# Local attention and a channel mix on one core: scores at the front of a slot, attention products behind the second key block, and TensorE's order as written

## The chip, the core and the metric

The kernel runs on one core of a Trainium2 chip. A core has a matrix engine (TensorE, PE in the rows), engines for elementwise work (VectorE, DVE; ScalarE, ACT; GpSimd, POOL) and SyncE (SP), whose queue issues the DMA transfers here. Each runs its own instructions in order and waits on semaphores for the others. The metric is the time of one execution in microseconds; lower is better.

## What is computed

Chunked local attention with a few memory keys, whose output goes through a token-shifting channel mix. Everything is float32, for 4 sequences of 768 tokens, 8 heads of 64 (512 channels) and a hidden width of 1024.

```
for each chunk of 32 queries:            # keys: 16 left, 32 own, 8 right, 8 memory = 64
    a = softmax(0.125 * q_c @ k_full.T)
    out_c = a @ v_full
x  = out, heads side by side             # (4, 768, 512)
xk = mu_k * x + (1 - mu_k) * x_prev      # x_prev: the token before
xr = mu_r * x + (1 - mu_r) * x_prev
k  = max(xk @ w_k, 0)
y  = sigmoid(xr @ w_r) * (k * k @ w_v)
```

## The kernel before

The work is cut into 12 units u of 256 tokens, each of two tiles of 128 tokens (tiles 2u and 2u+1). Each unit passes these blocks on TensorE, named here as in the code's tables:

- **s**: the scores of both tiles, 128 small products (line 465). VectorE takes the maximum and subtracts it, ScalarE takes the exponential, VectorE sums and normalizes.
- **a**: weights times values, one block for a tile (line 642), 64 products for the two. From unit 3 on (MOVED) the weights come to it by way of DRAM: VectorE transposes them in 32x32 squares (eT, line 708), SyncE stores them (eD, line 715), and four transfers load them into aTz (line 719). This is in `move`. ScalarE then copies the result into xT.
- **g0, g1**: the sigmoid's products (line 1141), and **h0 to h3**: the key products xk @ w_k (line 1252), 24 products each. Each operand is split into a high and a low part in a shorter float type, so each product is three: high by high, low by high, high by low. VectorE makes the mixes from the difference df of neighbouring tokens (lines 773 and 784); a cast gives the high part xh, a subtraction the low part xl (line 805). The mix for g is made first, the mix for h second.
- **p1 to p7**: the products with w_v (from unit 2 on), by a scheme of seven products instead of eight. Their operands (high parts ah, low parts al) are made of sums and differences of squared ReLUs. They gather in three banks: x (p1, then p2), z (p7, then p4) and y (p6, then p5, then p3). Between two products of a bank VectorE reads it. Three of these reads matter here: **u2** reads y after p6, and p5 waits for it; **c21** reads z after p4; **c22** reads y after p5, and p3 waits for it.

A **slot** u, as the word is used below, is the stretch of TensorE's work that holds h and p of unit u. It also holds g and a of unit u+1 and s of unit u+2.

What sets the order: the program doesn't write it out. Each operation goes into a `Plan` with its engine or alternatives, a cost and what it depends on. `te_order` gives each block of TensorE a due time by a written sequence. Then `Plan.turn` places the operations one by one on a modelled clock. For TensorE it takes only the first in the written sequence until STRICT (420) operations are placed. From then on it chooses among the next LOOK (400), so later blocks of TensorE can pass each other. The other engines' operations are placed among these, wherever the modelled clock has them first. A transfer's result counts as there DLAT (2.0 us) after its cost. The planner has no part in the run: it only fixes each engine's order. From about unit 3 on the order of TensorE that results is not the written one: h0 of the next unit stands ahead of p3, and p2 ahead of p5 or of h0.

Of the kernel before, what the change touches and what calls it, by code (L numbers as in the profile page):

```python
# [24 lines left out]
KT = DM // P  # L25
FT = DFF // P
# [1 line left out]
NEG = -3.0e38  # L28
TINY = 2.0**-112
LOOK = 400  # L30
STRICT = 420
EASE = 0.1
TURNS = 3
WHOLE = ("g0", "g1", "v0")
OWN = (1,)
PARTED = (1,)
LEAD = "s0.0.0 s0.0.1 s0.1 t0 t1 a0 s1.0 a1 h0.0.0 h0.0.1 h0.1.0 h0.2.0 h0.3.0 s1.1 h0.3.1 g0.0.0 g0.1.0 g0.0.1 h0.3.2 h0.3.3 g0.1.1 t2 t3 v0.0.0 a2 a3 v0.1.0 s2.0 v0.1.1 v0.0.1 h1.0.0 h1.0.1 h1.0.2 h1.0.3 h1.1.0 h1.1.1 t4 t5 h1.1.2 h1.1.3 a4 a5 v1.0.0 g1.0 g1.1 v1.0.1 g2.0 s3.0 g2.1 v1.1.0 v1.1.1"
UTOK = 256
FAST = 2
MOVED = 3  # L40
ROWS = [(0, 0, 1), (0, 1, 1), (1, 0, 2), (2, 0, 2), (3, 0, 2)]
QPU = UTOK // P
QKW = NPAIR * NJ * (CHUNK + NK)
VWW = NPAIR * NJ * D
HOP = {"pe": 0.22, "dve": 0.16, "act": 0.16, "pool": 0.16, "dma": 0.1}
SELF = {"pe": 0.0, "dve": 0.1, "act": 0.0, "pool": 0.1, "dma": 0.0}
DLAT = 2.0
# [25 lines left out]
class Slot:  # L73
    def __init__(self, tag):
        self.tag = tag
        self.users = []


class Op:

    def __init__(self, alts, fn, deps, new, use, due):
        self.alts = alts
        self.fn, self.new, self.due = fn, new, due
        self.deps = [d for d in deps if d is not None]
        self.eng = self.end = None
        self.rank = due if alts[0][0] == "pe" else None
        for s in list(new) + list(use):
            s.users.append(self)  # L90


class Plan:
# [4 lines left out]
        self.ops = []  # L98
        self.bufs = bufs

    def op(self, alts, fn, deps=(), new=(), use=(), due=1e9):
        fixed = isinstance(alts, tuple)
        if fixed:
            alts = [alts]
        o = Op([(a + (False,))[:3] for a in alts], fn, deps, new, use, due)
        o.seq, o.fixed = len(self.ops), fixed
        self.ops.append(o)
        return o

    def dues(self):  # L110
        for o in reversed(self.ops):
            for d in o.deps:
                e, c, _ = min(d.alts, key=lambda a: a[1])
                d.due = min(d.due, o.due - c - HOP[e] - (DLAT if e == "dma" else 0.0))

    def place(self, o, free, held):
        ready = [(d.end, d.eng) for d in o.deps]
# [44 lines left out]
    def turn(self, goal, ease):  # L162
        for o in self.ops:
            o.due = goal[o]
        self.dues()
        free, held, todo = {}, {}, {}
        for o in self.ops:
            todo.setdefault(o.alts[0][0], []).append(o)
        for q in todo.values():
            q.sort(key=lambda o: (o.rank if o.rank is not None else o.due, o.seq))  # L170
        done = []
        while len(done) < len(self.ops):
            best = None
            for e, q in todo.items():
                for o in q[: 1 if e == "pe" and len(done) < STRICT else LOOK]:
                    p = self.place(o, free, held)
                    if p is not None:
                        key = (p[1] + max(0.0, o.due - p[1]) * ease, o.due, o.seq)
                        if best is None or key < best[0]:
                            best = (key, o, p)  # L180
            _, o, p = best
            if o.rank is None and ease:
                o, p = self.filler(o, p, todo[o.alts[0][0]], free, held)
            _, t, eng, cost, port = p
            o.eng, o.start = eng, t
            free[eng] = t + cost
            if port:
                free["port"] = t + cost
            o.end = t + cost + (DLAT if eng == "dma" else 0.0)
            for s in o.new:  # L190
                held.setdefault(s.tag, []).append(s)
            todo[o.alts[0][0]].remove(o)
            done.append(o)
        done.sort(key=lambda o: (o.start, o.seq))
        return done


def te_order():

    nu = B * S // UTOK  # L200
    seq = [tuple([x[0]] + [int(n) for n in x[1:].split(".")]) for x in LEAD.split()]
    for u in range(1, nu):
        a, b = 2 * u + 2, 2 * u + 3
        g = [("g", u + 1, c) for c in range(QPU)]
        h = [("h", u, f) for f in range(FT // 2)]
        if u == 1:
            h = [("h", u, z, k) for z in range(2) for k in range(KT)]
        v = [("v", u, c, n) for c in range(QPU) for n in range(2)]
        n = 1 if u == nu - 2 else 2
        t = [("t", a), ("t", b)] * (u + 1 < MOVED)  # L210
        early = [("s", u + 2, 0)] * (u >= FAST)
        if u + 1 <= MOVED:
            seq += h[:n] + t + early + h[n : n + 1] + [("a", a), ("a", b)] + h[n + 1 :]
        else:
            seq += h[:1] + [("a", a), ("a", b)] + h[1:2] + early + h[2:]
        if u >= FAST:
            v = [("p", u, n) for n in (1, 7, 6, 4, 5, 2, 3)]
            if u >= nu - 2:
                g = [("g", nu - 1, u - (nu - 2))]
            if u == nu - 1:  # L220
                v = v[:3] + [("p", u, 4, 0), ("p", u, 5), ("p", u, 4, 1), ("p", u, 3), ("p", u, 2)]
            seq += v[:2] + g + v[2:]
            continue
        seq += v[:1] + [("s", u + 2, 0)] + g + v[1:]
    seq = list(dict.fromkeys(seq))
    last = {"t": B * NQT, "a": B * NQT}
    seq = [x for x in seq if x[1] < last.get(x[0], nu)]
    due, t = {}, 6.0
    for x in seq:
        assert x not in due  # L230
        due[x] = t
        t += PE_COST[x[0]] * (0.66 if x[:3] == ("h", 0, 0) else 0.33 if x[:3] == ("h", 0, KT - 1) else 1.32 if x[:2] == ("h", 0) else 0.5 if x[:2] == ("h", 1) else 1.32 if x[1] == 0 and f"{x[0]}{x[-1]}" in WHOLE else 1)
    return due
# [3 lines left out]
def local_attention__then__channel_mix(  # L237
# [24 lines left out]
    def sb(tag, shape, name, dt=F32):  # L262
        return work.tile(shape, dt, tag=tag, name=name, bufs=bufs.get(tag, 1))
# [19 lines left out]
    op = plan.op  # L283
    T = {}

    def copy(e, dst, src):
        if e is nc.scalar:
            e.copy(dst, src)  # L288
        else:
            e.tensor_copy(dst, src)  # L290
# [4 lines left out]
    qts = [(b, i) for b in range(B) for i in range(NQT)]  # L295
    units = [(b, u * UTOK) for b in range(B) for u in range(S // UTOK)]
    NU = len(units)
    due = te_order()
    chunks = [(w_k, wk_hl, k) for k in range(KT)]
    chunks += [(w_r, wr_hl, k) for k in range(KT // 2)]  # L300
# [309 lines left out]
    def attention(t, o_n, e):  # L610
# [39 lines left out]
        def f_x(e):  # L650
            if c == 0:
                x = T["xT", u] = sb("xT", [P, KT, 1 + UTOK], f"xT{u}")
                if units[u][1] == 0:
                    nc.gpsimd.memset(x[:, :, 0:1], 0.0)
                else:
                    nc.scalar.copy(x[:, :, 0:1], T["xT", u - 1][:, :, UTOK : UTOK + 1])
            copy(
# [42 lines left out]
    def move(u, o_n, e):  # L700

        X, M = NK // CHUNK * 2, NG // 2

        def f_turn():
            T["eT", u] = sb("eT", [P, NG * NK], f"eT{u}")
            nc.vector.transpose(
                T["eT", u].rearrange("p (x m q) -> p x m q", x=X, m=M),
                T["e", u].rearrange("p g k -> p (g k)").rearrange("p (m x k) -> p x m k", m=M, x=X),  # L710
            )

        def f_out():
            T["eD", u] = dram.tile([P, NG * NK], F32, tag="eD", name=f"eD{u}")
            nc.sync.dma_start(T["eD", u], T["eT", u])

        def f_in(x):
            s, z = x // 2, slice(CHUNK * x, CHUNK * (x + 1))
            nc.sync.dma_start(
                aTz[z, s].rearrange("p i n -> p (i n)").rearrange("p (j n) -> p j n", j=NJ),  # L720
                T["eD", u].rearrange("(j p) (x n) -> x p j n", j=NJ, x=X)[x],
            )

        ts, az, ds = Slot("eT"), [Slot("aT"), Slot("aT")], Slot("eD")
        o_t = op(("dve", 1.2), f_turn, [o_n], new=[ts], use=[e])
        o_free = prior["a"]
        o_o = op(("dma", 1.3), f_out, [o_t], new=[ds], use=[ts])
        landed = [op(("dma", 0.45), lambda x=x: f_in(x), [o_o, o_free], new=az * (x == 0), use=az * (x > 0) + [ds]) for x in range(X)]
        return landed, az

    mix = {}
# [6 lines left out]
    def prep_first(u):  # L738
        for m in range(2):
            fs = Slot("x4")  # L740
            done = {}
            for k, c, n in [(k, c, n) for k, c, n in ROWS if m == 0] or [(k, 0, QPU) for k in range(KT)]:
# [4 lines left out]
                def f_own(m=m, k=k, n=n, t=t, z=z, first=first):  # L747
                    if first:
                        T["xf", u, m] = sb("x4", [P, KT, UTOK], f"xf{u}_{m}")
                    x = T["px", t][:, k * P : (k + 1) * P] if n == 1 else T["xT", u][:, k, 1:]  # L750
# [652 lines left out]
    with tc.manual_schedule():  # L1403
        for o in plan.order():
            if o.eng == "pe":
                n = 0 if ("ph", 0, 0) in T else int((o.start - busy - 0.2) / (0.43 if busy else 0.86))
# [56 lines left out]
```

## Time and profile before

| | |
|---|---|
| time, median of 3 runs | 384.44 us (383.06 to 387.7) |
| time of the profiled execution | 382.86 us |
| its span | 380.9 us |
| TensorE busy | 372.1 us, 98% |
| VectorE busy | 308.5 us, 81% |
| ScalarE busy | 222.0 us, 58% |
| DMA, mean over the span | 153 GB/s |

Busy times are unions over an engine's instructions. Matrix products overlap, so TensorE's busy time doesn't say that it works at its peak; what it lost are the stretches in which nothing ran on it. Times of instructions are counted from the start of the span.

### The profile page before, as it was taken

How to read it: one execution, taken by the hardware profiler on the slowest of the kernel's cores; microseconds unless marked ns; L12 is line 12 of the kernel's file. 1: busy time of each engine (PE TensorE's matmuls, PEld its weight loads, DVE VectorE, ACT ScalarE, POOL GpSimd, SP SyncE). 2: the span in 40 equal slices, each digit the busy share in tenths (PEclk: the TensorE clock that was granted, in tenths of full speed). 3: DMA queues.
4: the chain of work that ended last, by engine and by line, in shares of the span. 5: the costliest groups of instructions: out<-in, count | busy, mean ns of one | idle time of the engine just before them, and what ended most of it. 6: DMA issues, size and time to landing. Idle time of an engine off the chain costs nothing.

```text
span 380.9 us, 10699 instructions
## 1 busy us (share of the span) xinstructions
PE 372.1 (98%) x4702; PEld 343.9 (90%) x4702; DVE 308.5 (81%) x496; ACT 222.0 (58%) x333; POOL 2.7 (1%) x11
## 2 busy tenths in 40 slices
PE   8999999999998999999999999999999999999996
PEld 6785589889998999999999999999999999999996
DVE  4899999989999499589498599599689689779264
ACT  2788998654771565456258349349249349355350
POOL 2000000000000000000000000000000000000000
PEclk9999999999999999999999999999999999999999
DMA  8999980323724431641650560570480440400101
GB/s 313 413 410 408 357 317 31 112 70 123 234 102 139 156 153 71 208 167 57 204 187 32 154 259 2 168 275 2 147 282 17 139 141 1 138 31 0 58 0 57
DMA packets 19822, 58.43 MB, mean 153 GB/s; under 512 B 2240, under 2 KB 7232, under 8 KB 19392
## 3 DMA queue, kind: packets, MB, share of 16 engines
q1 hardware_dynamic: 19776, 57.75, 42.5%
q8 instruction: 37, 0.61, 0.7%
q14 instruction: 9, 0.07, 0.1%
HBM read 46.73 MB, written 11.01 MB: 152 GB/s over the span
## 4 chain that ended last, share of the span: by engine, by line
PE 77%; DVE 10%; DMA 5%; ACT 4%; issue 2%; SPq 1%; DVEq 0%
PE ph L1252 26%; PE pr L1141 10%; PE accy L1043 6%; PE px L642 6%; PE accx L1043 4%; PE accz L1043 4%; PE pv L1354 4%; PE s L465 4%; PE ph L1198 4%; PE ph L1227 3%; DMA aTz<-eD 2%; DMA eD<-eT 2%; DVE al L988 2%; PE pr L1132 2%; PE pv L1341 2%
## 5 line engine op out<-in xcount | busy, mean ns | idle before, releaser
L1252 PE MATMUL ph<-xh,wk 128*128 128x256 f32 x320 | 89.7, 280 | 0.0
L1252 PE MATMUL ph<-xl,wk 128*128 128x256 f32 x320 | 88.2, 276 | 0.6 <-DVE xl L805 0.3
L1252 PE MATMUL ph<-xh,wl 128*128 128x256 f32 x320 | 88.0, 275 | 0.0
L1271 ACT ACTIVATE kf<-ph 128x512 f32<-128x512 f32 x48 | 28.6, 596 | 68.1 <-PE ph L1252 66.2
L1252 PEld LDWEIGHTS ph<-xh,wk 128*128 128x128 f32 x320 | 61.3, 192 | 1.4
L1252 PEld LDWEIGHTS ph<-xl,wk 128*128 128x128 f32 x320 | 61.4, 192 | 1.0 <-DVE xl L805 0.5
L1252 PEld LDWEIGHTS ph<-xh,wl 128*128 128x128 f32 x320 | 61.4, 192 | 0.0
L288 ACT CAST ah<-kf 128x512 fp32r<-128x512 f32 x47 | 29.0, 618 | 24.3 <-DVE kf L966 23.9
L988 DVE TENSOR_TENSOR al<-kf,ah 128x512 fp32r<-128x512 f32 x50 | 33.9, 682 | 3.7 <-ACT ah L288 3.4
L1141 PE MATMUL pr<-wr,xh 128*128 128x512 f32 x88 | 33.5, 381 | 0.0
L1141 PE MATMUL pr<-wr,xl 128*128 128x512 f32 x88 | 33.4, 379 | 0.0
L1141 PE MATMUL pr<-wl,xh 128*128 128x512 f32 x88 | 33.4, 379 | 0.0
L1278 ACT ACTIVATE kf<-kf 128x512 f32<-128x512 f32 x48 | 30.2, 631 | 1.4
L1085 DVE TENSOR_TENSOR o<-accy,o 128x256 f32<-128x256 f32 x30 | 12.4, 412 | 21.8 <-PE accy L1043 21.8
L773 DVE TENSOR_TENSOR df<-xT 128x1024 f32<-128x1024 f32 x10 | 12.2, 1224 | 18.9 <-ACT xT L288 18.9
L642 PEld LDWEIGHTS px<-aTz,vw 128*64 128x64 f32 x768 | 23.6, 138 | 4.3 <-PE accy L1043 1.9
L642 PE MATMUL px<-aTz,vw 128*64 128x64 f32 x768 | 25.2, 223 | 1.9 <-DMA aTz<-eD 1.4
L1043 PE MATMUL accx<-wv,ah 128*128 128x256 f32 x80 | 22.0, 275 | 0.0
L1043 PE MATMUL accx<-wl,ah 128*128 128x256 f32 x80 | 22.0, 275 | 0.0
L1043 PE MATMUL accx<-wv,al 128*128 128x256 f32 x80 | 22.0, 275 | 0.0
L288 ACT COPY xT<-px 128x512 f32<-128x512 f32 x24 | 14.1, 589 | 13.1 <-PE px L642 12.8
L288 ACT CAST ah<-st 128x512 fp32r<-128x512 f32 x18 | 11.1, 618 | 15.9 <-DVE st L966 15.7
(149 smaller groups left out, 959.1 us busy)
## 6 DMA issues: line engine op xcount, KB each, us to landing
qk<-in_qk_dram SPq DMA_DIRECT2D x23, 768.0 KB, 6.1
vw<-in_vw_dram SPq DMA_DIRECT2D x24, 512.0 KB, 4.8
out_dram<-o SPq DMA_DIRECT2D x23, 256.0 KB, 2.8
eD<-eT SPq DMA_DIRECT2D x9, 512.0 KB, 2.6
aTz<-eD SPq DMA_DIRECT2D x36, 128.0 KB, 2.9
raw<-in_w_v_dram SPq DMA_DIRECT2D x4, 1024.0 KB, 9.3
raw<-in_w_k_dram SPq DMA_DIRECT2D x3, 1024.0 KB, 13.1
raw<-in_w_r_dram SPq DMA_DIRECT2D x2, 1024.0 KB, 8.6
```

The source lines that it names most:

```text
L288: e.copy(dst, src)
L465: nc.tensor.matmul(s5[CHUNK * j : CHUNK * (j + 1), h, d - c, r, :], *operands(ts[d], r, j, slice(64 * h, 64 * h + 64)), start=True, stop=True,
L642: nc.tensor.matmul(p3[64 * h : 64 * h + 64, 2 * g : 2 * g + 2, CHUNK * j : CHUNK * j + CHUNK], v[:, g, h, j, :], a[:, h, g, j, :], start=True,
L988: nc.vector.tensor_sub(low(n), place[n](), T["ah", u, n].bitcast(F32))
L1043: nc.tensor.matmul(o, x, w, start=(n in fresh and c + i == 0), stop=(c == cs[-1] and i == 2), skip_group_check=True)
L1085: return lambda: nc.vector.tensor_add(out_part(*dst), acc(name), out_part(*src))
L1141: nc.tensor.matmul(pairs(p), x[:, k, c * P : (c + 1) * P], woven(w), start=(k + n == 0), stop=(k == KT - 1 and n == 2),)
L1198: nc.tensor.matmul(p[:, i * UTOK + c * P : i * UTOK + (c + n) * P], T["w", id(wk_hl[0]), k][:, fc], T["xf", u, 0][:, k, z], start=(i + k + ...
L1252: nc.tensor.matmul(pairs(p[:, i * UTOK : (i + 1) * UTOK]), w[:, fc], x[:, :, k].rearrange("p t n -> p n t"), start=(k + n == 0), stop=(k = ...
L1271: e.activation(part(), p, AF.Relu)
L1278: e.activation(q, q, AF.Square)
L1354: nc.tensor.matmul(pairs(p), x[:, tc_], woven(w), start=(f + n == 0), stop=(f == FT - 1 and n == 2),)
```

## The change

The constant STRICT becomes 9999, which is more than there are operations: TensorE's order is now the written sequence in full. That sequence is written anew for units 2 to 11, as a table of stages, in which "a" and "b" are the two a blocks of unit u+1. The latency that the planner counts for a transfer becomes a parameter of the operation: for the four loads of aTz it is 3.0 us for unit 3 and 6.0 us for the later ones, instead of 2.0.

```diff
-STRICT = 420
+STRICT = 9999
...
+STAGES = {
+    0: "s h0 h1 a b h2 h3 p1 p7 g0 g1 p6 p4 p5 p2 p3",
+    2: "h0 h1 s h2 a b h3 p1 p7 g0 g1 p6 p4 p5 p2 p3",
+    10: "h0 a b h1 h2 h3 p1 p7 g0 p6 p4 p5 p2 p3",
+    11: "h0 h1 h2 h3 p1 p7 g1 p6 p4a p5 p4b p3 p2",
+}
...
-                d.due = min(d.due, o.due - c - HOP[e] - (DLAT if e == "dma" else 0.0))
+                d.due = min(d.due, o.due - c - HOP[e] - (d.lat if e == "dma" else 0.0))
...
-            o.end = t + cost + (DLAT if eng == "dma" else 0.0)
+            o.end = t + cost + (o.lat if eng == "dma" else 0.0)
...
-        if u + 1 <= MOVED:
-            seq += h[:n] + t + early + h[n : n + 1] + [("a", a), ("a", b)] + h[n + 1 :]
-        else:
-            seq += h[:1] + [("a", a), ("a", b)] + h[1:2] + early + h[2:]
...
-            seq += v[:2] + g + v[2:]
...
+        seq += [own[x] for x in (STAGES[u] if u in STAGES else STAGES[0]).split()]
...
-        landed = [op(("dma", 0.45), lambda x=x: f_in(x), [o_o, o_free], new=az * (x == 0), use=az * (x > 0) + [ds]) for x in range(X)]
+        landed = [op(("dma", 0.45), lambda x=x: f_in(x), [o_o, o_free], new=az * (x == 0), use=az * (x > 0) + [ds], lat=6.0 if u > MOVED else 3.0) for x in range(X)]
```

How instructions move on the engines is shown at three places, with names that hold the unit (accx5 is bank x of unit 5, ph6_0 the block h0 of unit 6). Line numbers of the changed kernel are 5 lower.

On TensorE, the border of slots 5 and 6. Before, p2 of unit 5 ends, and h0 of unit 6 follows:

```order
L1043 MATMUL accx5_2662<-wv3_75,al2_5_2781 128x256
L1043 MATMUL accx5_2662<-wv3_75,ah2_5_2722 128x256
L1043 MATMUL accx5_2662<-wl8_561,ah2_5_2722 128x256
L1043 MATMUL accx5_2662<-wv3_75,al2_5_2781 128x256
L1252 MATMUL ph6_0_2817<-xh6_0_2726,wk0_68 128x256
L1252 MATMUL ph6_0_2817<-xl6_0_2783,wk0_68 128x256
```

Now, p3 of unit 5 ends, and the scores of unit 8 come before h0 of unit 6:

```order
L1038 MATMUL accy5_2751<-wl8_561,ah3_5_2768 128x256
L1038 MATMUL accy5_2751<-wv3_75,al2_5_2746 128x256
L460 MATMUL s8_0_2834<-qk16_2511 32x64 x32
L460 MATMUL s8_0_2834<-qk17_2515 32x64 x32
L1247 MATMUL ph6_0_2902<-xh6_0_2784,wk0_68 128x256
L1247 MATMUL ph6_0_2902<-xl6_0_2803,wk0_68 128x256
```

So p3 moved from behind h0 to in front of the border, and the scores from between h1 and h2 to the front of the slot.

On ScalarE, the start of slot 6 (kf6_0 is the ReLU and square of h0 and h1, e8 the softmax of unit 8). Before, ReLU and square of the key blocks come first, and the exponential behind all four:

```order
L1271 ACTIVATE kf6_0_2859<-ph6_1_2904 128x512
L1278 ACTIVATE kf6_0_2859<-kf6_0_2859 128x512
L288 CAST ah1_6_3006<-kf6_0_2859 128x512
L288 CAST ah7_6_3073<-st6_3041 128x512
L1271 ACTIVATE kf6_1_3075<-ph6_2_3010 128x512
L1278 ACTIVATE kf6_1_3075<-kf6_1_3075 128x512
L1271 ACTIVATE kf6_1_3075<-ph6_3_3045 128x512
L1278 ACTIVATE kf6_1_3075<-kf6_1_3075 128x512
L489 ACT_TABLE_LOAD
L489 ACTIVATE e8_3079<-e8_3079 128x1024
```

Now:

```order
L1266 ACTIVATE kf6_0_2961<-ph6_0_2902 128x512
L1273 ACTIVATE kf6_0_2961<-kf6_0_2961 128x512
L484 ACT_TABLE_LOAD
L484 ACTIVATE e8_2932<-e8_2932 128x1024
L1266 ACTIVATE kf6_0_2961<-ph6_1_2936 128x512
L1273 ACTIVATE kf6_0_2961<-kf6_0_2961 128x512
L651 COPY xT7_3005<-xT6_2586 128x4
L283 COPY xT7_3005<-px14_2969 128x4x128
L283 COPY xT7_3005<-px15_2988 128x4x128
L283 CAST ah7_6_3044<-st6_3012 128x512
L1266 ACTIVATE kf6_1_3078<-ph6_2_3014 128x512
L1273 ACTIVATE kf6_1_3078<-kf6_1_3078 128x512
```

The table load and the exponential moved from behind the fourth key block's square to behind the first's.

On VectorE, the end of slot 5 (eT7 is the transpose for unit 7, df6 the second mix of unit 6, o5 the output of unit 5). Before:

```order
L1082 TENSOR_TENSOR o5_1_2748<-accz5_2707,o5_0_2720 128x256
L708 STREAM_TRANSPOSE eT7_2764<-e7_2660 128x1024
L1085 TENSOR_TENSOR o5_1_2748<-accy5_2750,o5_0_2720 128x256
L988 TENSOR_TENSOR al2_5_2781<-kf5_1_2656,ah2_5_2722 128x512
L805 TENSOR_TENSOR xl6_0_2783<-df6_2512,xh6_0_2726 128x1024
L1085 TENSOR_TENSOR o5_1_2748<-accz5_2707,o5_1_2748 128x256
L966 TENSOR_TENSOR kf5_1_2656<-kf5_1_2656,st5_2623 128x4x128
L1085 TENSOR_TENSOR o5_1_2748<-accy5_2750,o5_1_2748 128x256
L1108 TENSOR_TENSOR o5_1_2748<-o5_1_2748,sg5_2325 128x512
```

Now:

```order
L703 STREAM_TRANSPOSE eT7_2744<-e7_2513 128x1024
L983 TENSOR_TENSOR al2_5_2746<-kf5_1_2659,ah2_5_2700 128x512
L961 TENSOR_TENSOR kf5_1_2659<-kf5_1_2659,st5_2593 128x4x128
L779 SCALAR_TENSOR_TENSOR df6_2627<-df6_2627,mu_sb_67,xT6_2586 128x256 x4
L1080 TENSOR_TENSOR o5_1_2719<-accy5_2751,o5_0_2698 128x256
L983 TENSOR_TENSOR al2_5_2746<-kf5_1_2659,ah3_5_2768 128x512
L1080 TENSOR_TENSOR o5_1_2719<-accz5_2685,o5_1_2719 128x256
L800 TENSOR_TENSOR xl6_0_2803<-df6_2627,xh6_0_2784 128x1024
L1080 TENSOR_TENSOR o5_1_2719<-accy5_2751,o5_1_2719 128x256
L1103 TENSOR_TENSOR o5_1_2719<-o5_1_2719,sg5_2324 128x512
```

The first add that reads accy5 is u2, the second c22. Before, u2 stood right behind the transpose, and the second mix (the four instructions of line 784) far ahead of these rows. Now an al, a combination and the four mix instructions stand between transpose and u2, and the xl that is made of that mix stands between u2 and c22.

## Rows read from the trace of the kernel before

**Rows 1.** The page, part 1: busy us (share of the span) xinstructions
```profile
PE   372.1 (98%) x4702; PEld 343.9 (90%) x4702; DVE 308.5 (81%) x496; ACT 222.0 (58%) x333; POOL 2.7 (1%) x11
```

**Rows 2.** TensorE's waits, whole span: us in total, times, longest
```profile
PE px L642 <- DMA aTz<-eD: 1.4, 3, 0.5
...
PE accy L1043 <- DVE o L1085: 0.7, 2, 0.5
PE s L465 <- issue: 0.6, 1, 0.6
...
PE ph L1252 <- DVE xl L805: 0.3, 1, 0.3
PE ph L1252 <- issue: 0.2, 1, 0.2
```

**Rows 3.** Timeline, slot 2: start, us, engine, line, instruction [idle before <-releaser]
```profile
116.74 0.38 DVE L1085 TENSOR_TENSOR o<-accy,o 128x256 f32<-128x256 f32 x1
...
117.27 0.35 PE L1043 MATMUL accy<-t1h,ah 128*128 128x256 f32 x1 [0.50 <-DVE o L1085]
```

**Rows 4.** Chain of waits, slot 6: start, us, what (times)
```profile
274.11 2.02 PE px L642 x64
276.12 2.88 PE ph L1252 x24
279.00 1.41 PE s L465 x89
280.41 5.55 PE ph L1252 x48
285.96 1.34 PE accx L1043 x12
...
303.20 0.84 PE px L642 x23
```

**Rows 5.** Timeline of ScalarE, slot 6
```profile
286.00 0.60 ACT L1271 ACTIVATE kf<-ph 128x512 f32<-128x512 f32 x1 [0.78 <-PE ph L1252]
286.63 0.63 ACT L1278 ACTIVATE kf<-kf 128x512 f32<-128x512 f32 x1
287.28 1.28 ACT L489 ACT_TABLE_LOAD   x1
288.57 1.06 ACT L489 ACTIVATE e<-e 128x1024 f32<-128x1024 f32 x1
...
291.87 1.55 ACT L288 CAST xh<-df 128x1024 fp32r<-128x1024 f32 x1
```

**Rows 6.** Casts: line 290's (ns, min/median/max), and the group on ScalarE (us, mean ns)
```profile
L290 DVE CAST ah<-kf x3: 415/419/421, 119.6 to 367.8; 128x512 fp32r<-128x512 f32 x3
...
L288 ACT CAST xh<-xf 128x1024 fp32r<-128x1024 f32 x3 | 3.1, 1049 | 0.0
```

**Rows 7.** Timeline of VectorE, slot 6
```profile
286.19 1.66 DVE L784 SCALAR_TENSOR_TENSOR df<-df,mu_sb,xT 128x256 f32<-128x256 f32 x4
...
289.66 1.22 DVE L493 TENSOR_REDUCE sum<-e 128x16 f32<-128x1024 f32 x1 [0.60 <-ACT e L489]
...
291.29 0.63 DVE L988 TENSOR_TENSOR al<-st,ah 128x512 fp32r<-128x512 f32 x1
...
292.43 1.22 DVE L499 TENSOR_TENSOR e<-e,sum 128x1024 f32<-128x1024 f32 x1
293.57 0.68 DVE L988 TENSOR_TENSOR al<-kf,ah 128x512 fp32r<-128x512 f32 x1
294.17 0.42 DVE L1082 TENSOR_TENSOR o<-accz,o 128x256 f32<-128x256 f32 x1
294.50 1.23 DVE L708 STREAM_TRANSPOSE eT<-e 128x1024 f32<-128x1024 f32 x1
...
296.56 1.34 DVE L805 TENSOR_TENSOR xl<-df,xh 128x1024 fp32r<-128x1024 f32 x1
```

**Rows 8.** The page, part 6: loads of vw, KB each, us from issue to landing
```profile
vw<-in_vw_dram SPq DMA_DIRECT2D x24, 512.0 KB, 4.8
```

More of the change, by code (lines that the diff above doesn't have):

```diff
@@ L79, with __init__ @@
 class Op:
-    def __init__(self, alts, fn, deps, new, use, due):
+    def __init__(self, alts, fn, deps, new, use, due, lat):
         self.alts = alts
@@ L87, in __init__ @@
         self.eng = self.end = None
+        self.lat = lat
         self.rank = due if alts[0][0] == "pe" else None
@@ L99, in __init__, with op @@
         self.bufs = bufs
-    def op(self, alts, fn, deps=(), new=(), use=(), due=1e9):
+    def op(self, alts, fn, deps=(), new=(), use=(), due=1e9, lat=DLAT):
         fixed = isinstance(alts, tuple)
@@ L104, in op @@
             alts = [alts]
-        o = Op([(a + (False,))[:3] for a in alts], fn, deps, new, use, due)
+        o = Op([(a + (False,))[:3] for a in alts], fn, deps, new, use, due, lat)
         o.seq, o.fixed = len(self.ops), fixed
@@ L202, in te_order @@
     for u in range(1, nu):
-        a, b = 2 * u + 2, 2 * u + 3
-        g = [("g", u + 1, c) for c in range(QPU)]
-        h = [("h", u, f) for f in range(FT // 2)]
-        if u == 1:
[L207 to L211, printed above, removed]
-        if u + 1 <= MOVED:
-            seq += h[:n] + t + early + h[n : n + 1] + [("a", a), ("a", b)] + h[n + 1 :]
-        else:
-            seq += h[:1] + [("a", a), ("a", b)] + h[1:2] + early + h[2:]
[L216 to L221, printed above, removed]
-            seq += v[:2] + g + v[2:]
+        own = {f"h{f}": ("h", u, f) for f in range(FT // 2)}
+        own.update({f"p{n}": ("p", u, n) for n in range(1, 8)})
+        own.update({f"g{c}": ("g", min(u + 1, nu - 1), c) for c in range(QPU)})
+        own.update({"p4a": ("p", u, 4, 0), "p4b": ("p", u, 4, 1)})
+        own.update(a=("a", 2 * u + 2), b=("a", 2 * u + 3), s=("s", u + 2, 0))
+        if u == 1:
+            seq += [("h", u, z, k) for z in range(2) for k in range(KT)]
+            seq += [("v", u, c, n) for c in range(QPU) for n in range(2)]
             continue
-        seq += v[:1] + [("s", u + 2, 0)] + g + v[1:]
+        seq += [own[x] for x in (STAGES[u] if u in STAGES else STAGES[0]).split()]
     seq = list(dict.fromkeys(seq))
```

## The prediction

> **What bounds the kernel now.** I read the busy shares first: TensorE is busy for 98% of the span and VectorE for 81% [rows 1]. A kernel like this can win only what TensorE waits, and it loses whatever it makes TensorE wait for. So I read next, in the list of TensorE's waits, what those are [rows 2]. The products of attention weights and values (a) waited three times, 1.4 us in all, for the softmax on its way through DRAM. Accumulating products waited twice, 0.7 us, for VectorE to read the bank (both in slot 2). A key product waited 0.3 us for VectorE's low part xl. 0.8 us are "issue", with no wait that the profile shows. That is little over 3 us. A wait costs a little more than is listed: twelve products take 1.34 us, 0.11 each [rows 4], while the first one after a wait lasts 0.35 us [rows 3], so some 0.2 us of overlap is lost with each.
>
> Then I read the chain of waits in slot 6, where TensorE alone is the chain. From one a to the next it takes 303.20 - 274.11 = 29.09 us [rows 4], and nothing is lost. This is the pattern of slots 6 to 9.
>
> **What the change does.** No instruction of TensorE is added or removed. Three things move.
>
> *Scores to the front of the slot, a behind h1.* In slot 6 the scores end at 280.41 and the next a starts at 303.20 [rows 4], so the softmax has 22.8 us. That is where the three a waited by some 0.5 us: the path needs about 23.3. Afterwards scores end 1.41 us into a slot, and the next a starts a full slot later, behind scores and two key blocks: 29.09 + 1.41 + 5.55 - 1.41 = 34.6 us. That leaves 11 us to spare, so these waits go: 1.4 + 3 x 0.2 = 2.0 us. Scores now also stand between the last product of slot 2 and the first key block of slot 3. They take 1.41 us, more than the wait of 0.3 us for xl there: another 0.3 + 0.2. Gain: **2.5 us**. On SP's queue the two loads of vw now stand behind those of qk. A vw load lands 4.8 us after its issue [rows 8] and has some 27 us until the next a, so I cost this at nothing; without that cover a would wait up to 4.8 us. The six counted for landing instead of two changes only the planner's clock, and shows here only as the new order.
>
> *Exponential early on ScalarE.* It moves from behind the fourth key block to between the first and second. This sets what VectorE does next.
>
> *p5, p2, p3 one behind the other.* Before, h0 of the next slot stood ahead of p3 and gave VectorE 2.68 us. Now p3 must follow p2 at once, and it waits for two instructions of VectorE: the add c22 that empties bank y after p5, and the low part of operand 3. Likewise p5 waits for the add u2, which reads y after p6. That was so before; what changes is when VectorE gets there. I add up its queue from rows, with 0 at the end of the last product of the slot before. On VectorE an instruction that needs nothing of its neighbour follows 0.08 us before that one's end (an al lasts 0.68 and the next starts 0.60 later; an add 0.33 later [rows 7]).
>
> - ScalarE: h0 ends at 1.41 + 2.88 = 4.29 [rows 4]. ReLU follows 0.04 later (286.00 behind 285.96), square 0.63 later, table load 0.65, exponential 1.29, which lasts 1.06 [rows 5]. It ends at **7.96**; the table load cannot run earlier, as it stands behind ReLU and square.
> - VectorE from 7.99 on, without a gap until xl: the three sum instructions 1.63 (289.66 to 291.29), a cast (0.42 us [rows 6], less 0.08) 0.34, difference and al 1.20, df 1.25 (a 128x1024 instruction of 1.22, as normalizing [rows 7], on which the next depends), four mixes 1.66: 14.07.
> - xh is now cast by ScalarE, 1.05 us [rows 6], so xl starts at 15.20. xl and normalizing 2 x 1.14, two combinations 1.20, the add behind p7 0.33, three al 1.80, the transpose 1.16, an al and a combination 1.20, four mixes 1.66: **24.83** [rows 7].
> - p5 would start at 29.09 - 3 x 1.34 = 25.07. u2 starts at 24.75 and lasts some 0.4, and 0.15 us lie between such an add and the product that waits for it (116.74 + 0.38 to 117.27 [rows 3]): 25.30. p5 waits 0.23, plus 0.2 for the overlap.
> - xh of the other mix takes ScalarE 1.55 us [rows 5], so xl starts at 26.46. It lasts 1.34 [rows 7], and c22 follows at 27.72. With 0.42 for c22 and 0.15, p3 starts at 28.29. It would have come at 29.09 - 1.34 + 0.43 = 28.18, so it waits 0.11, plus 0.2.
>
> A slot so loses **0.7 us**. The same order stands in slots 3 to 8, six times: 4.2 us. In slot 9 the transpose goes into the gap before xl's operand and a cast moves to VectorE, so c22 comes some 0.7 us earlier; I count 0.1. Slots 10 and 11 have no softmax, and there VectorE has the time. The first score bank and the g products are early enough (xl ends at 16.4; g0 comes at 17.2).
>
> Both ends: if every hand-over between engines takes the 0.15 us of [rows 3] instead of 0.04, the six on this path add 0.7, and a slot loses 1.4. If they come 0.7 earlier in all, a slot loses nothing. The 0.8 us of "issue" I leave in place, since the change does not touch what they show; they could go too.
>
> **Sum.** 382.86 (the profiled execution, 380.9 of it the span) - 2.5 + 4.2 + 0.1 = 384.7, that is +1.8 us. The profiled time lies 1.6 under the median of the three runs, 384.44; the middle of all four times is 383.75, and on this I put it: **385.5 us**.
>
> **The rivals.**
> 1. VectorE is in time and nothing new waits. Then the change gives what it removes: 383.75 - 2.5 = 381.3, or 380.5 without the "issue". For it: in slot 6 u2 stands behind the transpose too and nothing waits there [rows 4, 7], and VectorE is idle for 4 us early in the slot. Against: those 4 us lie ahead of the exponential, and cannot be moved behind it. It decides if c22 ends 0.7 us earlier than I have it.
> 2. More waits, 1.4 us a slot by the longer hand-overs: 383.75 - 2.5 + 8.4 + 0.4 = 390.0. For it: slot 2 has the order p5, p2, p3 already, and lost both accumulating waits [rows 2] there. Against: slot 2 also turns weights on VectorE.
> 3. The exponential ends later still, by the length of a table load, 1.28 us [rows 5]: 0.7 + 1.28 in six slots and 1.1 in slot 9 are 13, so 383.75 - 2.5 + 13 = 394.3. Against: ScalarE idles early in the slot, and in [rows 5] the exponential starts 0.01 us behind the load. The Trainium skill (ScalarE: Activation LUTs, "What ACT_TABLE_LOAD costs") gives 1283 ns for the load and some 1380 ns of drain, 2.66 us for each change of set. By that page the exponential would end 1.4 us later, and it would come out near this rival. The trace agrees on the load and shows no drain.
> 4. The change doesn't do what it says: the a still wait as before, for vw or for the transfers behind it on SP, and VectorE is in time: 383.75 - 0.5 = 383.2.
>
> **How the numbers follow.** Forecast 0.50 (its own range, 0.4 to 1.0 us a slot: 383.5 to 387.4), rival 1 0.23, rival 2 0.15, rival 3 0.04, rival 4 0.08. The range 381 to 389 takes in the forecast, rival 4, most of rival 1 and the lower part of rival 2. Within 2% (about what a measurement of this kernel can tell from no change) is 376.8 to 392.1. Faster than that is out of reach, as all waits of TensorE after slot 1 are some 4 us: 0.01. Slower needs rival 3 or the far end of rival 2: 0.05.
>
> **What would show it.** The a should wait for no transfer, and the wait for xl at the start of slot 3 should be gone. Slots 3 to 8 should be 29.7 to 29.9 us each, with an accumulating product waiting for VectorE's adds once or twice in each; the exponential should end some 8 us into the slot. I am wrong if slots 3 to 8 take 29.1 us (rival 1), if g or p6 waits, or if a still does.

## The result, and the profile after

The change takes 387.39 us (median of 20 runs, 385.64 to 388.55) beside 384.54 us of the kernel before (20 runs on the same chips). The ratio is 1.0066, 95% interval 1.0048 to 1.0084: slower by 1.8 to 3.2 us, within the 2% that the chances went by. The profiled execution took 387.26 us, 385.1 of it the span (before: 382.86 and 380.9). Lines of the code stand 5 lower than before (L1043 is now L1038).

The page's part 1, and from its part 4 the engines' shares of the chain that ended last:

```profile
PE 373.8 (97%) x4702; PEld 344.9 (90%) x4702; DVE 307.3 (80%) x495; ACT 223.7 (58%) x334; POOL 2.7 (1%) x11
...
PE 54%; DVE 29%; ACT 8%; DMA 4%; issue 4%; SPq 1%; ACTq 0%; DVEq 0%
```

TensorE has as many instructions as in [rows 1]; it waits longer. For what, its waits say (us in total, times, longest):

```profile
PE accy L1038 <- DVE o L1080: 3.5, 8, 0.5
PE s L460 <- issue: 1.2, 2, 0.7
...
PE px L637 <- DMA aTz<-eD: 0.9, 1, 0.9
PE accy L1038 <- ACT xh L283: 0.5, 1, 0.5
```

Against [rows 2]: the three waits of a product a in slots 3 to 5 are gone, and so is that of a key product for xl. Accumulating products now wait eight times for an add, once in each slot from 2 to 9; a ninth wait, of 0.1 us, falls in slot 10. The wait of 0.9 us for aTz is a new one, in slot 2. The last line is p3's wait in slot 2 for a cast of ScalarE.

The chain of waits in slot 6 (start, us, what) no longer stays on TensorE as it did in [rows 4]:

```profile
214.63 1.41 PE s L460 x89
216.05 2.89 PE ph L1247 x24
...
219.02 0.61 ACT kf L1266
...
220.29 1.28 ACT L484
...
221.59 1.07 ACT e L484
...
222.68 1.23 DVE sum L488
...
238.11 1.58 DVE df L779 x4
239.69 0.34 DVE o L1080
...
240.17 1.58 PE accy L1038 x12
```

Behind h0 it goes to ScalarE (ReLU, square, table load, exponential), from 222.68 on through VectorE's queue (with ScalarE's cast of xh in it), and back to TensorE at p5. That is the path which the prediction had added up. Its end in the timeline, VectorE and then TensorE:

```profile
222.68 1.22 DVE L488 TENSOR_REDUCE sum<-e 128x16 f32<-128x1024 f32 x1 [3.91 <-ACT e L484]
...
229.83 1.23 DVE L800 TENSOR_TENSOR xl<-xf,xh 128x1024 fp32r<-128x1024 f32 x1 [0.51 <-ACT xh L283]
...
238.03 1.66 DVE L779 SCALAR_TENSOR_TENSOR df<-df,mu_sb,xT 128x256 f32<-128x256 f32 x4
239.62 0.41 DVE L1080 TENSOR_TENSOR o<-accy,o 128x256 f32<-128x256 f32 x1
...
242.25 0.41 DVE L1080 TENSOR_TENSOR o<-accy,o 128x256 f32<-128x256 f32 x1
```
```profile
240.17 0.35 PE L1038 MATMUL accy<-t1h,ah 128*128 128x256 f32 x1 [0.46 <-DVE o L1080]
```

The add at 239.62 is u2, and p5 follows 0.14 us behind its end. The add at 242.25 is c22. It ends at 242.66, and p3, which starts at 242.92 behind p2, does not wait for it.

**Where the 4.3 us went.** I compare the starts of equal blocks of TensorE in the two traces: the p6 of the last slot starts at 374.62 us instead of 370.35.

| | us |
|---|---|
| p5 waits in slots 3 to 8: p4's block 1.96 or 1.97 instead of 1.34, p5's 1.41 instead of 1.34, six times 0.70 | +4.2 |
| the same in slots 9 (0.43) and 10 (0.33) | +0.76 |
| three a waits gone (p3's blocks of 1.96, 1.99, 1.97 became 1.43) | -1.63 |
| xl's wait at the start of slot 3 gone (block of 3.38 became 2.68) | -0.70 |
| "issue" in slots 3 to 5: 1.85 instead of 1.39 | +0.46 |
| a's wait in slot 2 | +1.02 |
| everything else up to slot 2's end | +0.13 |
| sum | +4.24 |

### The profile page after: what moved, and what is told of

It is laid out like the page before. It is cut to its first block, busy times and chain, and to the rows that moved or that the text cites. A ratio compares the mean times of both kernels' runs of the same rounds, so it can differ in the third digit from the quotient of the medians.

```text
span 385.1 us, 10692 instructions
## 1 busy us (share of the span) xinstructions
PE 373.8 (97%) x4702; PEld 344.9 (90%) x4702; DVE 307.3 (80%) x495; ACT 223.7 (58%) x334; POOL 2.7 (1%) x11
## 4 chain that ended last, share of the span: by engine, by line
PE 54%; DVE 29%; ACT 8%; DMA 4%; issue 4%; SPq 1%; ACTq 0%; DVEq 0%
PE ph L1247 14%; PE accy L1038 8%; DVE al L983 6%; PE accx L1038 4%; PE pv L1349 4%; PE pr L1136 4%; PE ph L1193 4%; PE s L460 4%; DVE df L779 3%; DVE xf L779 3%; PE px L637 3%; DMA vw<-in_vw_dram 3%; PE ph L1222 3%; DVE eT L703 2%; DVE sum L488 2%
## 5 line engine op out<-in xcount | busy, mean ns | idle before, releaser
L488 DVE TENSOR_REDUCE sum<-e 128x16 f32<-128x1024 f32 (+1 forms) x12 | 14.1, 1174 | 27.8 <-ACT e L484 27.7
L283 ACT CAST ah<-kf 128x512 fp32r<-128x512 f32 x41 | 25.4, 621 | 18.3 <-DVE kf L961 17.8
L1038 PE MATMUL accx<-wv,al 128*128 128x256 f32 x80 | 22.0, 275 | 0.0
L1038 PE MATMUL accx<-wl,ah 128*128 128x256 f32 x80 | 22.0, 275 | 0.0
L1038 PE MATMUL accx<-wv,ah 128*128 128x256 f32 x80 | 22.0, 275 | 0.0
L460 PEld LDWEIGHTS s<-qk 64*32 64x32 f32 x1472 | 15.5, 105 | 4.4 <-issue 3.3
L460 PE MATMUL s<-qk 64*32 64x64 f32 x1472 | 17.9, 225 | 1.2 <-issue 1.2
```

The costliest lines, as they stand in the source:

```text
L460: nc.tensor.matmul(s5[CHUNK * j : CHUNK * (j + 1), h, d - c, r, :], *operands(ts[d], r, j, slice(64 * h, 64 * h + 64)), start=True, stop=True,
L488: nc.vector.reduce_sum(sm, grid(T["e", u], c, n), axis=AX.X)
L1038: nc.tensor.matmul(o, x, w, start=(n in fresh and c + i == 0), stop=(c == cs[-1] and i == 2), skip_group_check=True)
```

## The experiments

The kernel before was run beside each: 384.5 us beside the runs on the landing time, the table load, the written order alone and the free order, 383.3 beside the last, 383.5 beside the others. Where an expectation counts runs, these four are the first to the fourth; the sum twice and the normalizing are the fifth and sixth, the four kernels with small or quick products the seventh to the tenth.

**The sum over the keys twice.** In f_sum:

```
+                if u >= 5:
+                    nc.vector.reduce_sum(sm, grid(T["e", u], c, n), axis=AX.X)
```

> The change, with softmax's sum over the keys (1.22 us on VectorE, ahead of u2 in the same slot) issued twice for units 5 to 11, which stand in slots 3 to 9; nothing else moves, and what is computed is the same. Theory A (VectorE's chain up to u2 sets when p5 starts, with no room left): each of the seven slots grows by about 1.2 us, the p5 wait from 0.46 us to about 1.7 us, and the span from 385.1 to about 393 us. Rival B (the longer slots come from something that VectorE's lateness does not set, such as TensorE's own instruction supply or the loads): the span stays within 1 us of 385.1. Rival C (VectorE's and ScalarE's rows are late together, but p5 waits for ScalarE): at most half of 1.2 us per slot, span 389 us or less.

Span 393.3 us, 8.2 more than the change's; the one execution took 395.1. TensorE's first wait:

```profile
PE accy L1040 <- DVE o L1082: 9.3, 8, 1.4
```

From the g products of slot 6 to those of slot 7 it takes 31.06 us instead of 29.80: the second sum arrives with 1.26 us, in full, at TensorE. Rivals B and C fall. Seven times 1.25 would be 8.75; slot 2's wait for aTz is missing in this execution.

**Normalizing one column.** In f_norm:

```
+                if u >= 5:
+                    e = e[:, :, :, 0:1]
```

> The change, with the normalizing of units 5 to 11 (1.21 us on VectorE, ahead of u2) done for one key column instead of 64, so about 1 us less on VectorE ahead of u2 in slots 3 to 9; the rest of the normalizing is left out. Theory A: the p5 waits (0.62 us of slot length in each of slots 3 to 8, 0.36 in slot 9) go, the undisturbed slots come to 29.2 us, and the span falls from 385.1 to about 381 us. Rival B: the p5 waits or the slot length of 29.8 us stay, span within 1 us of 385.1.

Span 380.0 us in one execution, a fall of 5.1. The p5 waits of slots 3 to 10 are gone (4.96 us in the table above) and the wait for aTz is missing here too (1.0), while the start up to slot 2 took 0.55 us longer and a slot stays 0.07 above 29.10. The stalls within the score blocks changed too: 1.12 us in slot 4 and none in slot 5, instead of 0.79 and 0.96. Of the accumulating products' waits only the two of slot 2 stay:

```profile
PE accy L1040 <- ACT xh L283: 0.5, 1, 0.5
PE accy L1040 <- DVE o L1082: 0.5, 1, 0.5
```

The table by stretches, one line for each of two slots (from g to g; busy us of each engine):

```profile
199.68:228.84 29.16, 29.16 (x399) 28.11 (x398) 22.74 (x41) 16.55 (x26) 0.00 (x0) 1.00 0.44 146
228.84:258.02 29.18, 29.18 (x398) 28.14 (x397) 22.78 (x41) 16.58 (x26) 0.11 (x1) 1.00 0.43 145
```

The same for the change:

```profile
201.90:231.69 29.79, 29.33 (x398) 28.12 (x397) 23.71 (x40) 16.67 (x26) 0.00 (x0) 1.00 0.42 143
231.69:261.48 29.79, 29.33 (x398) 28.13 (x397) 23.73 (x40) 16.68 (x26) 0.10 (x1) 1.00 0.41 142
```

In the third column TensorE stands idle for 0.46 us in a slot of the change (29.79 less 29.33) and for nothing without that 1 us of VectorE's work. Theory A is shown from both sides.

**The time counted for landing undone.** In the plan of the softmax loads:

```
-  ..., use=az * (x > 0) + [ds], lat=6.0 if u > MOVED else 3.0) for x in range(X)]
+  ..., use=az * (x > 0) + [ds]) for x in range(X)]
```

TensorE's order stays as in the change; the planner's order on VectorE and SP does not.

> The change with the latency parameter left at 2.0 us for the loads of aTz; TensorE's order is that of the change, instruction for instruction. What moves is VectorE's queue: normalizing comes just ahead of u2 and the transpose behind it, where the change has both before the combination and the mixes. Theory A (p5 waits because the transpose and others stand ahead of u2): one transpose of 1.16 us less and one al of 0.60 more ahead of u2, so u2 ends some 0.55 us earlier and p5's wait of 0.46 us in slots 3 to 8 falls to 0.1 or less; 6 x 0.5 = 3.2 us less than the change, a ratio to before of 0.998 to 1.001. Theory B (the loss lies in TensorE's new order itself, whatever VectorE's queue is): as the change, 1.006 to 1.008. The a could wait again if the later transpose lands late: it has some 11 us to spare, so neither theory expects it.

388.89 us, ratio 1.0108 (1.0070 to 1.0146), span 387.9: in time a miss for theory A. Its p5 waits did fall, to 0.1 us or nothing in slots 3 to 8, as it has them; but a waits again. For the a of slot 3 (VectorE, then SP's issues, then TensorE's total):

```profile
121.83 1.24 DVE L703 STREAM_TRANSPOSE eT<-e 128x1024 f32<-128x1024 f32 x1
```
```profile
123.09 1.37 SPq L710 DMA_DIRECT2D eD<-eT  x1
125.20 0.34 SPq L1083 DMA_DIRECT2D out_dram<-o  x1
127.23 2.61 SPq L714 DMA_DIRECT2D aTz<-eD  x4
```
```profile
PE px L637 <- DMA aTz<-eD: 3.5, 3, 2.4
```

The change issues that transpose at 116.70 us and the loads from 120.59 on. Here they come 5.1 and 6.6 us later, and a, at 132.51, waits 2.36. So the parameter does more than move a clock: by it the planner chooses how early VectorE does the transpose and how late u2. The prediction had costed it at nothing beyond the order at hand, which holds for the change; but a's 11 us to spare exist only because VectorE transposes early, and that is what p5 pays for.

**The table load counted.** The planner counts 1.28 us for a table load at unit 2's exponential alone; here at every one.

```
-            o_e = op(("act", 0.15 + 0.85 * w + 1.28 * (u == 2)), f_exp, [o_b], use=[es])
+            o_e = op(("act", 0.15 + 0.85 * w + 1.28 * (u >= 2)), f_exp, [o_b], use=[es])
```

> The change with the planner counting 1.28 us for ScalarE's table load at the exponential of every unit from 2 on (it counts it for unit 2 alone). TensorE's order stays; on VectorE u2 comes ahead of the four mixes, and the sums behind the combinations. Theory A: u2 is 1.58 us earlier, p5 does not wait, a slot of 3 to 8 takes 29.1 to 29.3 us instead of 29.8, ratio 0.997 to 1.001. Theory B: as the change, 1.006 to 1.008.

387.23 us, ratio 1.0059 (1.0025 to 1.0093), span 386.4: no gain, and a miss for theory A in time. Yet the p5 waits went in slots 3 to 6 and 9, and slot 6 fell to 29.23 us. The timeline of VectorE there shows why:

```profile
240.85 0.65 DVE L961 TENSOR_TENSOR kf<-kf,st 128x512 f32<-128x512 f32 x1
241.42 0.41 DVE L1080 TENSOR_TENSOR o<-accy,o 128x256 f32<-128x256 f32 x1
241.75 1.66 DVE L779 SCALAR_TENSOR_TENSOR df<-df,mu_sb,xT 128x256 f32<-128x256 f32 x4
```

u2 now stands ahead of the four mixes and not behind them, as in the change (238.03 and 239.62). What this won was lost to something else:

```profile
PE s L460 <- issue: 3.5, 2, 1.8
```

The score blocks of slots 4 and 5 took 3.29 and 3.50 us instead of 1.41. That asked for a theory of its own (F, below). The key block behind the second took 7.18 us instead of 5.55, and for another reason: TensorE waits nowhere in it. From 188.2 to 191.6 us the trace has a granted clock of 0.50, the lower level (1.2 GHz), and 1.0 before and after. TensorE had stood still for 1.85 us in the score block, up to 187.31. The page's row (40 slices of 9.7 us, in tenths) shows it as an 8:

```profile
PEclk9999999999999999999899999999999999999999
```

So of the 5.9 us of issue stalls that two expectations below speak of, 1.6 are the clock's. It doesn't fall in every execution: four of the ten, at a mean granted clock of 0.995, took 387.5 to 389.7 us, the other six, at 0.999 or 1.0, 384.2 to 387.6.

**TensorE's order as written, alone.** The kernel before with one number changed:

```
-STRICT = 420
+STRICT = 9999
```

> The kernel before with only STRICT raised: TensorE in the old written order (h0, a, h1, s, h2, h3, p1, p7, g0, g1, p6, p4, p5, p2, p3), scores in the old place. VectorE has u2 behind an al and the transpose. Theory A: the softmax still has 22.8 us, so a waits some 0.5 us in some slots, and u2 comes some 0.4 us late for p5 in slots 3 to 8: 1.005 to 1.012 of before. Theory B (the scores' place or p5, p2, p3 in a row): if the scores' place costs it, 0.998 to 1.002; if the row of three, 1.006 to 1.008.

389.85 us, ratio 1.0125 (1.0086 to 1.0165). The old place of the scores is kept, and still p5 and p3 wait in every slot from 3 to 9:

```profile
PE accy L1043 <- DVE o L1085: 4.2, 16, 0.5
```

So this part of the change alone costs more than the whole (388.97 to 390.56 us beside 385.64 to 388.55). In the kernel before, the planner had moved h0 of the next slot ahead of p3; the written order takes that cover away.

**The change without that part.** Its order of stages and its landing times, with STRICT back at 420:

> The change with STRICT left at 420: new table and latencies, but the planner may again let blocks of TensorE pass. It puts p2 between p4 and p5, h0 of the next unit ahead of p3, and the scores behind p7. Theory A: u2 has a block of 1.34 us more until p5 and c22 one of 2.68 us until p3, the a have time, so only the waits of slot 2 and the issue stay: 0.993 to 0.999. Theory B (scores early cost what they gain, by what they put on VectorE): 1.003 to 1.008.

382.27 us, ratio 0.9935 (0.9907 to 0.9963): 0.4 to 0.9% faster than the kernel before, and faster than the change. From slot 4 on the planner puts the scores behind p7 and, in most slots, p2 ahead of p5 and h0 ahead of p3. The profiled execution lost 2.0 us to a load of qk, some 7 us from the start, and slot 4's score block stalled by 1.02 us.

**The place of the scores in TensorE's instruction stream.** All "issue" stalls within a score block, in every trace, look alike. The page's part 3 for the change has 37 packets on the instruction queue for 9404 instructions of TensorE (4702 products, 4702 loads of weights), 254 for each:

```profile
q8 instruction: 37, 0.61, 0.7%
```

A score block has 256 instructions in 1.41 us; twelve products with their loads, 24 instructions, take 1.34 us elsewhere. In all the traces together there are 22 such stalls of over 0.2 us behind slot 2, and each time the stalled product follows 2.3 to 2.7 us behind the start of such a packet (in the kernel before 192.27 behind 189.85). Theory F: TensorE has run out of instructions, and whether it does depends on where in a stretch of 256 the block starts. Two kernels put 56 small products on zeros into the start:

```
+                for _ in range(56 * (o.rank == third)):
+                    nc.tensor.matmul(warm[:P, :4], zero_sb[:, :P], zero_sb[:, :4], start=True, stop=True)
```

> The change, with 56 matmuls of 4 columns on zeros put into TensorE's idle time at the start, which move every later TensorE instruction by 112 places in its instruction stream; every other row is the same. Theory F (the issue stalls inside the s blocks of slots 4 and 5 come from where a 256-instruction block of TensorE's stream ends inside the 256 quick instructions of s; those two s blocks start at place 172 and 196 of a block, and shifted at 28 and 52, where no kernel so far showed a stall): the two stalls of 0.8 and 0.95 us go, the span falls to about 383.5 us. Rival D (the stalls come from the transfers that run in slots 4 and 5): they stay where they are and the time stays within 0.5 us of the change's. A stall that turns up in another slot at a place near 172 to 220 speaks for F too. The start may grow by up to 1 us if the extra matmuls do not fit the idle time.

> The kernel of the second run (the change with the table load's 1.28 us counted for every unit's exponential, profile of 386.4 us with 5.9 us of issue stalls in slots 3 to 5) with the same 56 small matmuls at the start. Theory F: its issue stalls go, at least those inside s (3.7 us with places 172 and 196), and the time falls from 387.2 us to about 381.5 to 383.5 us, below the kernel before. Rival D (transfers): the issue stalls of 5.9 us stay, time within 1 us of 387.2 us.

Both missed in time: 406.78 and 407.44 us, ratios 1.0610 (1.0551 to 1.0670) and 1.0621 (1.0578 to 1.0664). I had the small products wrong twice. Each counts as two of TensorE's, so they shift the stream by 224 places, not 112; and they are slow (ns, min/median/max):

```profile
L1407 PE MATMUL warm<-zero_sb x112: 169/354/354, 7.3 to 26.3; 128*128 128x4 f32 x112
```

They hold the start up by 19 us. The page's row of the granted clock (40 slices of 10.1 us, in tenths) goes with that:

```profile
PEclk9658999999999999999999999999999999999999
```

With nothing but these products on it from 7.3 us on, TensorE was granted 0.5 to 0.6 from 10 to 30 us, the lower level for most of it. At the upper level one of them started every 0.11 us, at the lower (354 ns each) every 0.21. Behind the start the traces can be read. A shift of 224 puts s at 164 and 188 in slots 5 and 6 rather than at 172 and 196 in slots 4 and 5, and there the stalls went. Next, 27 quick products (64 rows, 32 by 64) with 100 places, and without the lost start:

> The change with 27 quick matmuls (64 rows, 32 by 64, on zeros) in the idle time at the start in place of two slower ones, which moves every later TensorE instruction by 100 places; all else as in the change. With places counted as in the traces, the s blocks of slots 2 to 9 then start at 64, 248, 16, 40, 64, 88, 112 and 136 of a 256-instruction stretch, all outside the places of 164 to 220 at which s blocks stalled so far. Theory F (the stall goes by the place of s in the instruction stream): no issue stall in any s of slots 3 to 9, the span falls from 385.1 to about 383.4 us, the median from 387.4 to about 385.5 us. Rival D (it goes by the transfers of slots 4 and 5): those two stalls stay, and the time with them. The p5 waits of theory A stay in both.

> The kernel of the second run (table load counted for every unit) with the same 27 quick matmuls. Theory A says that its p5 waits are gone but for some 0.9 us, theory F that its issue stalls (5.9 us in slots 3 to 5, 3.7 of them inside s) now go too: span from 386.4 to about 380.5 to 382.5 us, median 381.5 to 384 us, below the kernel before (384.5). Rival D: stalls of 3.7 to 5.9 us stay in slots 4 and 5, time 386 to 388 us.

390.66 us, ratio 1.0174 (1.0144 to 1.0203), and 387.54 us, ratio 1.0113 (1.0073 to 1.0154): in time a miss for F. In the traces slots 4 and 5 are free of stalls in both kernels, for the first time with these orders. But others appeared where F had none. In the first kernel they are within slot 3's score block (2.06 us), in slot 9's (0.70) and in the first key products (a block of 15.58 us at 17.41, in the change 11.73). In the second the first key products stood still for 1.8 us. The waits of the first:

```profile
PE s L460 <- issue: 2.2, 2, 1.8
PE ph L1193 <- issue: 2.1, 1, 2.1
```

Behind both the granted clock was 0.50 for 3.4 us (from 21.6 and from 130.9 us), and slot 3's first key block took 7.18 us instead of 5.56, as above with the table load. Stalls, lower clock and a start that is 0.75 us longer make 9.0 us. Gone are the stalls of slots 4 and 5 and the wait for aTz, 2.8 together. That is the 6.2 us by which the span of 391.3 us is longer than the change's.

All kernels whose score blocks stand at the front of the slot or at the old place throughout, places counted from the traces, time beyond 1.41 us in parentheses:

```
kernel                slot 3     slot 4      slot 5      slot 6      slot 9
before                116 (0)    140 (0)     164 (.88)   188 (0)     4 (0)
change                148 (0)    172 (.79)   196 (.96)   220 (0)     36 (0)
change again          148 (0)    172 (.75)   196 (.72)   220 (0)     36 (0)
sum twice             148 (0)    172 (1.01)  196 (.69)   220 (0)     36 (0)
one column            148 (0)    172 (1.12)  196 (0)     220 (0)     36 (0)
written order alone   116 (0)    140 (0)     164 (.83)   188 (0)     4 (0)
landing undone        148 (0)    172 (.52)   196 (.71)   220 (1.20)  36 (0)
table load counted    148 (0)    172 (1.88)  196 (2.09)  220 (0)     36 (0)
56 small products     116 (0)    140 (0)     164 (.67)   188 (1.03)  4 (0)
same + table load     116 (0)    140 (0)     164 (1.77)  188 (1.58)  4 (0)
27 quick products     248 (2.06)  16 (0)      40 (0)      64 (0)     136 (.70)
same + table load     248 (0)     16 (0)      40 (0)      64 (0)     136 (1.05)
```

In slots 4 to 6 every stall sits between 164 and 220, in whichever slot that falls. That they follow the stream is shown, and rival D as the only cause falls. The place alone does not decide (188, 196, 220 and 248 stall in one kernel and not in another); what else does, such as transfers at the same time, is open. That TensorE runs out of instructions is how I read the 2.3 to 2.7 us behind a packet; no run shows it directly.

**The free order with the table load counted.** Both one-line edits from above.

> The fourth run's kernel (TensorE's order free again behind its first part, 382.3 us) with the table load counted for every unit; its s blocks come out at places 220, 148, 148, 28, 52, 76, 100 and 124, none of which stalled in a slot behind 3 so far. Theory A: the last p5 wait (0.62 us in slot 3) goes; theory F: the issue stall of 1.0 us in slot 4 goes. Together the span falls from 380.5 to about 379 us, the time from 382.3 to 380.5 to 381.5 us, some 0.8 to 1% below the kernel before. If neither holds it stays at 382.3 us.

381.00 us (379.60 to 381.37), ratio 0.9928 (0.9910 to 0.9946), span 379.1, although slot 2 lost 1.3 us to aTz in the profiled execution. No score block stalled, and from slot 3 on no accumulating product waits. The chain of waits there stays on TensorE:

```profile
206.37 1.34 PE accy L1038 x12
207.71 1.34 PE accz L1038 x12
209.04 1.34 PE accx L1038 x12
210.38 1.34 PE accy L1038 x12
211.72 2.68 PE ph L1247 x24
214.41 1.34 PE accy L1038 x12
```

These are p6, p4, p2, p5, h0 and p3, here and in the three slots that follow: u2 has p4 and p2 as cover, c22 has h0. It is the best version found, though it does not stand apart from the 382.27 us of the free order alone: the intervals overlap.

**The change again**, for a second trace:

> The change once more, unaltered, for a second trace. Theory G (the 0.95 us for which the first attention product of slot 2 waited for its transposed weights from DRAM belongs to that one execution, since the kernels of the fifth, sixth and ninth run have the same code there and no such wait): the wait is gone or of another size, the span with it at about 384.1 us; the eight p5 waits of 0.46 us (0.1 to 0.2 in slots 9 and 10) and the two issue stalls of 0.7 to 1.0 us in slots 4 and 5 are there again. Rival H (it belongs to the change): a wait of 0.8 to 1.0 us again, span 385.1 us.

Span 384.2 us. The p5 waits stand as before (3.5 us, eight times), the score blocks of slots 4 and 5 take 2.16 and 2.13 us, and a does not wait in slot 2. G holds: that wait of 0.95 us belongs to single executions, not to the change.

## Why the prediction was right, and where it was not

**The verdict and the mechanism held.** TensorE waits in slots 3 to 8 because the exponential sits behind h0 on ScalarE and VectorE's whole queue behind it ends too late for p5. Both doses show it: 1.25 us more on that queue cost 1.26 a slot, 1 us less took the wait away. Slots 6 to 8 take 29.8 us, as foretold; slots 4 and 5, with stalls in their score blocks, take 30.6 and 30.8. In slot 6, with 0 at the end of the last product of slot 5 (214.63), the exponential ended at 8.03 us (7.96 predicted), xl started at 15.20 (15.20), u2 at 24.99 (24.75) and p5 at 25.54 (25.30).

**0.7 us a slot was right as a sum and wrong in its parts; that the sum came out is luck.** I had 0.43 for p5 and 0.31 for p3. Measured are 0.70 and nothing. Two terms were mis-sized, and the errors cancel:

- From xl to u2 VectorE took 9.79 us where I had summed 9.55. Most of it is one al and one combination that followed the instruction before them after 0.72 and 0.69 us instead of 0.60. This falls on p5, and so p3 could not come before 28.29 us, where I had 28.18.
- For the cast of the other mix I took 1.55 us from [rows 5]. In the changed order the same cast took 1.24 to 1.27 us in slots 3 to 8. In slot 6 (ScalarE's cast, then VectorE's xl):

```profile
239.73 1.25 ACT L283 CAST xh<-df 128x1024 fp32r<-128x1024 f32 x1 [0.46 <-DVE df L779]
241.01 1.33 DVE L800 TENSOR_TENSOR xl<-df,xh 128x1024 fp32r<-128x1024 f32 x1
```

So c22 ended at 28.03 and would have let p3 start at 28.2, while p5's wait had already put it at 28.3. With a cast of 1.55 us p3 would have waited some 0.2 us more (an estimate: 0.30 less the 0.12 between these two). Why the cast is shorter here is open.

**Slots 9 and 10 were mis-sized**: 0.1 us predicted, 0.76 measured. In slot 9 I looked at c22 alone; u2 stands behind a combination and a cast there and p5 waits 0.43. In slot 10 I argued that VectorE has time without a softmax. It has, but the planner put xl (1.32 us, from 352.73) right ahead of u2 (353.97), so the order made it late. The forecast's own range has a slip as well: 0.4 us a slot gives 383.75 at its lower end, not 383.5.

**The gain held**: 2.33 us instead of 2.5. No a waits in slots 3 to 11, and the wait for xl is gone. Cost 0 for vw behind qk held: no a from slot 3 on waits for vw.

**"Issue" left in place** was nearly right for this kernel (+0.46 us), but the ground was not. I wrote that the change does not touch what those stalls show. They follow the place of the score blocks in the instruction stream, which the change moves. With the same order on TensorE the score blocks lost 1.5 us in one trace (the change again) and 4.0 in another (table load counted), where the lower clock behind one of them cost 1.6 more.

**The time** came out 1.9 us above 385.5. The starting point I took, 383.75, lies 0.8 under the median of the kernel before; slots 9 and 10 make 0.66, issue 0.46 and the gain 0.17. That is 2.1. Rival 1 fell with the p5 waits. Rival 2's longer hand-overs were seen in part (0.24 of 0.7 us a slot), and rival 4 fell with the a waits. Rival 3 fell with the exponential, 0.01 us behind its table load.

## What to carry to other kernels

Work that is moved earlier on one engine can make another engine's queue the critical chain: add up the queue from the event that starts it to each read that frees a bank, and let the first wait absorb what the later ones would add. Whether a later read waits at all can hang on 0.1 us, and a price taken from another place in the queue (1.55 us for a cast that took 1.25) decides it. A position in a hand-written order that looks like filler (a key block between two accumulating blocks) may be the cover of such a read; freeze the order only with that cover in it. And a latency number given to a planner changes what it puts first on other engines: here the transpose moved by 5 us with nothing else edited.

## What the runs showed of the hardware

TensorE can stand still in a dense block with no wait that the profile shows. Score blocks lost 0.5 to 2.1 us each at a mean granted clock of 0.97 to 1.0. The Trainium skill (Runtime: NRT & Kernel Launch, "Instruction fetch mechanics") says that instructions come in blocks of 256 and that the cost of passing from one to the next is mostly hidden. The packet count agrees with the first (254 instructions each); for 256 instructions in 1.41 us, stalled 2.3 to 2.7 us behind the start of a packet, the second does not always hold here.

Such a stall can cost twice. Behind 1.85 us of standing still (table load counted), 1.78 and 2.15 us (27 quick products) the granted clock was 0.50 for 3.4 us, and twice a key block took 7.18 us instead of about 5.55. Behind waits of 2.36 us for aTz (landing time undone) and 1.81 us in the first key products (quick products with the table load) it stayed at 1.0, so what decides is open.

Products of 4 columns on 128 rows are not quick, and a run of them did not keep the clock: one started every 0.11 us at the upper level, as often as products of 256 columns do [rows 4], and every 0.21 at the granted clock of 0.5 to which it fell, while 54 of 64 rows by 32 took 0.98 us in all. And ScalarE's cast of the other mix took 1.25 us in slot 6 of the change and 1.55 in [rows 5], for the same shape.
